# A transformer block with adaptive LayerNorm on one core: loads begun once per step, a fourth exp bank in some half-steps, and another order of the V tiles in the ramp

## The chip, the cores and the metric

The kernel runs on one core of one Trainium2 chip. The metric is the device time of one execution in microseconds (us); less is better. A core has five engines with instruction queues of their own: TensorE (PE in the profile, its weight loads PEld), VectorE (DVE), ScalarE (ACT), GpSimd (POOL) and SyncE (SP). SP only starts transfers here, one after the other, in the order of the program.

## What is computed

The input `x` has 2048 rows of 512 numbers, all in fp32. A vector `c` gives two shifts, two scales and two gates:

```python
mod = (_silu(c) @ w_mod).reshape(c.shape[0], 6, 1, -1)
sa, ca, ga, sb, cb, gb = (mod[:, i] for i in range(6))
h = _layernorm(x) * (1 + ca) + sa
x = x + ga * _A_ref(h, A_wqkv, A_wo)          # attention, 32 heads of 16 dims, no mask
h = _layernorm(x) * (1 + cb) + sb
x = x + gb * _B_ref(h, B_w1, B_b1, B_w2, B_b2)  # 512 -> 1792, gelu (tanh form), -> 512
```

Attention takes a softmax over all 2048 keys for each query, with the scale 1/4 on the scores.

## The kernel before

**Numbers.** Every fp32 operand of a large product is split into a high and a low part, and three products (high by high, low by high, high by low) are added in one PSUM bank. For the scores of a head of 16 dims the three are stacked along the contraction: 48 rows, and for the exp two more rows that carry minus the row maximum. So a score tile is one matmul, `mx` (line 393) with 48 rows and `e` (line 577) with 50.

**Units and half-steps.** Attention is cut into 32 units: 4 blocks of 512 queries by 8 groups of 4 heads. A unit has 16 steps of 128 keys. TensorE works on two halves of its rows, `a` = 0 and 1, with two heads of the unit in each. The loop runs over 512 pieces that the code calls half-steps (`half_step`, 16 to a unit); each is as long as a step, and from one to the next the row half in which a background product runs changes. A half-step has on TensorE:

- 4 matmuls `e`, whose exp ScalarE takes into tiles `p` (line 582). They go round the PSUM banks 0, 1 and 2.
- 4 matmuls `mx` for a later unit, whose maxima over 512 keys VectorE takes (line 398). They go round the banks 3, 4 and 5. When a unit's 64 reductions are done, `max_rows` turns them into rows and sends them over DRAM into the rows 48 and 49 of that unit's Q tile (`qst`, line 423).
- 4 matmuls `pv` (line 606): probabilities by V with a column of ones, into bank 6, one bank for the 16 half-steps of a unit. At a unit's end ScalarE copies it to `osb` (line 594), which goes to DRAM (`ou`).
- Where there is any, up to 6 matmuls of a background product into bank 7 (ring `bg`). In the first block of queries these are the Q and K projections of the later head groups (`block0`); then for each finished block the output projection, the second LayerNorm and the FFN (`ffn_block`).

A clock of the program, `clock["t"]`, counts exp tiles; `later(n, f)` writes the instructions of `f` down n ticks on. So the order on each engine is fixed when the program is built.

**Loads.** `step_start(s)` is called by `exp_mm` as a step begins. In step 1 of a unit it loads the first half of the keys of the unit after the next (`load_k`, line 364, 6 transfers into `kh`), in step 2 that unit's Q (`load_q`, line 379, 6 transfers into `qst`), in step 3 the next unit's V (`load_v`, line 529, one transfer into `vg`), in step 9 the second half of the keys. Every third step it also prepares a piece of the FFN's weights (`prep`), and it calls `try_prep`. The condition by which `exp_mm` calls it is

```python
if min(ec) == ec[a] and ec[a] % 2 == 0 and (a == 0 or ec[0] > ec[1]):
    step_start(s)
```

where `ec` counts the `e` of the two row halves; it is met a second time when the other half reaches the same step with the two counts level.

**The attention output.** `o_prep` (four times for a block) loads the row sums `dn` (line 636) and the outputs `ob` (line 639) back from DRAM. Ten ticks later VectorE takes the reciprocal of `dn` (line 646), which goes to DRAM and comes back spread over the rows as `rb`; GpSimd divides (line 658). The FFN's pools open (`open_ffn`) when the list of weights to prepare is empty, and `o_prep` begins after that.

**The ramp.** Ahead of the loop the four blocks of 512 rows go through: the first LayerNorm (`ln1`: statistics on VectorE, the factor by a power on GpSimd, line 232, scaling on ScalarE, line 249), its transposes (`ln1_t`: TensorE line 260, ScalarE line 266, high and low parts on GpSimd, lines 268 and 269, on VectorE too for the first block), the K projection (`proj_qk`, stored by line 308 and loaded back by `load_k`), and four V tiles (`proj_v`). From the second block on the V tiles are written as a `quad`: four groups in two banks' worth of row halves, with pairs of `mx` put between their matmuls, 2, 1, 1, 2, 1, 1, 2 and 1 pairs after every sixth index. The rows of block b lie in `xin[b % 2]`. After the last block a quad of K projections and the rest of 88 `mx` follow, and then the loop.

**The tail.** After half-step 511 the last block's output projection and FFN run by themselves.

Of the kernel before, what the change touches and what calls it, by code (L numbers as in the profile page):

```python
# [17 lines left out]
D = 512  # L18
# [4 lines left out]
KC = D // P  # L23
NB = 4
# [25 lines left out]
def block_kernel(ctx: ExitStack, tc: tile.TileContext, x, wqkv, wo, w1, b1, w2, b2, c, w_mod, out):  # L50
# [84 lines left out]
    def stage(name):  # L135
        return spool.tile([P, D], F32, tag="s2", name=name, bufs=4)
# [8 lines left out]
    def load_wm(i, slot):  # L145
        sy.dma_start(wslot[slot], wm_r[:, :, i * D : (i + 1) * D])

    def load_x(b):
        for t in range(4):
            r0 = b * TB + t * P  # L150
            sy.dma_start(xin[b % 2][:, t], x[r0 : r0 + P, :])
# [17 lines left out]
                ac.activation(t[:, 0, w], raw[:, w], AF.Copy)  # L169
                gp.tensor_tensor(t[:, 1, w], raw[:, w], t[:, 0, w].bitcast(F32), op=ALU.subtract)  # L170

    def load_split_v():
        for i in range(KC):
            r = stage("vraw")
            sy.dma_start(r, wq_r[:, i, 2 * D :])
            ac.activation(wv[:, 0, i], r, AF.Copy)
            eng = gp if i % 2 else ve
            eng.tensor_tensor(wv[:, 1, i], r, wv[:, 0, i].bitcast(F32), op=ALU.subtract)
# [3 lines left out]
    load_wm(1, 0)  # L182
    load_wm(0, 1)
    load_w(0)
    load_x(1)


    ac.activation(s_c, c_c, AF.Exp, scale=-1.0)
# [243 lines left out]
    def mx_pair():  # L432
        seen = [f() for f in [mx_mm(1), mx_mm(0)]][0]
        advance()
        return seen
# [4 lines left out]
    rows = ln1(0)  # L440
# [7 lines left out]
    mrow = mod_copy(psm)  # L448
    mod_cols(0, mrow)
    ev()  # L450
    load_split_v()
    sy.dma_start(one_d.rearrange("a (x y) -> a x y", y=128), ones[:, None, :].to_broadcast([2, HS // 128, 128]))
    def quad(groups, visits):

        at = [take(bk) for _, bk, _ in groups]
        seen, visits = {}, iter(visits)
        for phase in range(2):
            for two in ((0, 1), (2, 3)):
                for m in range(12):
                    for i in two:  # L460
                        h = phase ^ (i % 2)
                        terms = groups[i][0]
                        ins = mm(at[i], terms[m], 12 * phase + m, 24, slice(h * 64, h * 64 + 64)).ins
                        if phase and not m:
                            tc.add_manual_dep(ins, seen[two].name, AFTER, reason="both halves of the rows add to one bank")
                        if phase and m == 11:
                            groups[i][2](at[i])
                    if m % 6 == 5:
                        for n in range(next(visits)):
                            ins = mx_pair()  # L470
                            if not n and m == 11:
                                seen[two] = ins.ins

    for b in range(NB):
        if b + 1 < NB:
            rows = ln1(b + 1)
        run(proj_qk("pr", 1, 0, b, fast=True))
        if b == 0:
            run(proj_qk("pr", 0, 0, 0, fast=True))
        for u in range(2):  # L480
            if u == 0 or b < 2:
                load_k(u, b // 2, (b % 2) * TB, (b % 2 + 1) * TB)
            if b == 0:
                load_q(u)
        if b + 2 < NB:
            load_x(b + 2)
        if b == 0:
            load_w(1)
            load_wm(4, 0)
            load_wm(3, 1)  # L490
        if b + 1 < NB:
            ln1_t(b + 1, rows)()
        if b == 1:
            split_w(1)
            psm = take("pr")
            mod_part(psm, 0)
            mod_part(psm, 1)
            mrow = mod_copy(psm)
            mod_cols(1, mrow)
            load_wm(2, 0)  # L500
            load_wm(5, 1)
        if b == 3:
            psm = take("pr")
            mod_part(psm, 0)
            mod_part(psm, 1)
            mrow = mod_copy(psm)
            mod_bcast((ga_b, gb_b), mrow)
        tiles = [proj_v("pr", b, t) for t in range(4)]
        if b:
            quad(tiles, (2, 1, 1, 2, 1, 1, 2, 1))  # L510
        else:
            for t in tiles:
                run(t)
        if b + 1 == NB:
            sy.dma_start(b2_b, bass.AP(tensor=b2.tensor, offset=b2.offset, ap=[[0, P], [1, D]]))
            sy.dma_start(b1_h, b1.rearrange("(f p) -> p f", p=P))
# [12 lines left out]
        sy.dma_start(vg[u], v_d[u % NG])  # L529

    load_v(0)
    quad([proj_qk("pr", 1, 1, b) for b in range(NB)], (2, 1, 1, 2, 1, 1, 2, 1))
    run(proj_qk("pr", 0, 1, 0))
    ac.activation(b1_h, b1_h, AF.Copy, scale=0.5)
    gp.tensor_tensor(b2_b, b2_b, gb_b, op=ALU.mult)
# [25 lines left out]
    ring("mx", (3, 4, 5))  # L561
    ring("pv", (6,))
    ring("bg", (7,))
    ec = [0, 0]
    cur = {"pv": 0}

    def exp_mm(a):

        s, p = divmod(ec[a], 2)
        if min(ec) == ec[a] and ec[a] % 2 == 0 and (a == 0 or ec[0] > ec[1]):  # L570
            step_start(s)
        ec[a] += 1
        u, kc = divmod(s, NKC)
        assert u in mrows, (u, ec, xc, red, clock["t"])
        r0 = a * 64
        ps = take("e")
        te.matmul(ps, kh(u, kc // 8)[r0 : r0 + KX, p, (kc % 8) * P : (kc % 8 + 1) * P], qst[u][r0 : r0 + KX, p],  # L577
                  start=True, stop=True)

        def act():  # L580
            t = ppool.tile([P, TB], F32, tag="p", name="p")
            saw(ac.activation(t, ps, AF.Exp, scale=SCALE))  # L582
            pt[4 * s + p * 2 + a] = t
            advance()

        return act
# [302 lines left out]
    def half_step(hs):  # L889
        h = hs % 2  # L890
        if h:
            wload()
        if act["g"] is None:
            j = next(jobs, None)
            if callable(j):
                j()
            elif j is not None:
                act["g"] = {"group": j, "at": [0, 0], "n": 0, "seen": None}
        nx = min(64 * NU, LEAD + 4 * (hs + 1))
        ne = 4 * (hs + 1)  # L900

        def x_ok(a):
            return sum(xc) < nx and xc[a] < 32 * NU

        def e_ok(a):
            return sum(ec) < ne and ec[a] < 2 * NU * NKC

        more = act["g"] is not None
        k = 0
        while more and k < RUN:  # L910
            a = 1 - h
            more = bg_mm(h)
            if e_ok(a) and sum(ec) < ne - 1 and (k % 2 == 1 or not x_ok(a)):
                exp_mm(a)()
            elif x_ok(a):
                mx_mm(a)()
            k += 1
        while sum(ec) < ne or sum(xc) < nx:
            a = 0 if ec[0] <= ec[1] else 1
            fs = []  # L920
            if sum(ec) < ne:
                fs.append(exp_mm(a))
                if x_ok(1 - a):
                    fs.append(mx_mm(1 - a))
                elif e_ok(1 - a):
                    fs.append(exp_mm(1 - a))
            else:
                fs += [mx_mm(i) for i in range(2) if x_ok(i)]
            for f in fs:
                f()  # L930
        if hs:
            assert min(ec) >= 2 * cur["pv"] + 2
            pv_step()
# [86 lines left out]
```

## Time and profile before

| | |
|---|---|
| three runs | 1872.36, 1882.72, 1886.42 us |
| median | 1882.72 us |
| profiled execution | 1873.15 us, of which the span of the trace is 1871.3 |
| mean granted TensorE clock | 0.966 of full |
| busy: PE, DVE, ACT, POOL | 1757.6, 1404.0, 1212.9, 601.3 us |
| as shares of the span | 94%, 75%, 65%, 32% |
| transfers | 279.09 MB, 149 GB/s on the mean |

The costliest groups of instructions, with the idle time ahead of them and what ended most of it:

```profile
L398 DVE TENSOR_REDUCE mxp<-mx 128x1 f32<-128x512 f32 x2048 | 1273.6, 681 | 222.9 <-PE mx L393 192.1
L582 ACT ACTIVATE p<-e 128x512 f32<-128x512 f32 x2048 | 1070.3, 603 | 397.8 <-PE e L577 334.3
L393 PE MATMUL mx<-kh,qst 48*128 48x512 f32 x2048 | 877.2, 446 | 37.3 <-DVE mxp L398 36.4
L577 PE MATMUL e<-qst,kh 50*128 50x512 f32 x2048 | 761.9, 425 | 25.2 <-ACT p L582 17.3
L606 PE MATMUL pv<-p,vg 128*32 128x512 f32 x4096 | 557.6, 617 | 0.0
```

How to read such rows. A group's row has its line, engine, operation, the tile written and the tiles read with partitions and elements, the count, then busy microseconds, mean nanoseconds of one, and the idle time of the engine just before. Busy times of TensorE add up instructions that overlap in its pipeline, so its share says little by itself. A row of one instruction begins with its start and its duration in microseconds; in brackets stand the engine's idle time just before it and what ended that. The row of a stretch (`440.00:462.00`) has its length, then for PE, PEld, DVE, ACT and POOL the busy time and in brackets the number of instructions, then the granted TensorE clock, the busy share of the transfer engines and the GB/s. The chain (the row of `PE 76%`) follows the last instruction back, at each step to what released it. DMA rows with SPq have the start and the time on SP's queue.

### The profile page before, as it was taken

The page shows a single profiled execution, that of the slowest core. Times are in us where ns is not written, and L with a number is a line of the kernel's source. Part 1 is how long each engine was busy: PE and PEld are TensorE (multiplying, and loading weights), DVE is VectorE, ACT ScalarE, POOL GpSimd, SP SyncE. Part 2 cuts the span into 40 slices and gives each one's busy share as a digit, 9 for nine tenths or more (in the row PEclk, how much of TensorE's full clock was granted, in tenths as well). Part 3 has the DMA queues.
Part 4 walks back from the last instruction along what each step waited for, and adds up shares of the span by engine and source line. Part 5 has one row for each costly group of instructions (what it writes and reads, how often), then busy time and mean ns, then how long its engine had stood idle before and what let it go on. Part 6 is the DMA issues. An engine that isn't in the chain of part 4 may idle for free.

```text
span 1871.3 us, 32540 instructions
## 1 busy us (share of the span) xinstructions
PE 1757.6 (94%) x12032; PEld 905.2 (48%) x12032; DVE 1404.0 (75%) x2347; ACT 1212.9 (65%) x2303; POOL 601.3 (32%) x640
## 2 busy tenths in 40 slices
PE   7698999998888899999999989999999999999899
PEld 5465444443333444444444444444444444444677
DVE  4466888887787978888888988888889878860232
ACT  3223777777565678778766668777776668777031
POOL 3213545442100146405510046504510046504520
PEclk8898999999899999999999999999999999999899
DMA  5828778777775467767767754435547457612544
GB/s 168 245 84 203 200 195 215 198 205 158 187 152 111 109 131 158 146 113 181 177 138 175 197 115 109 98 87 142 115 91 194 75 135 159 146 61 91 186 158 157
DMA packets 135292, 279.09 MB, mean 149 GB/s; under 512 B 34598, under 2 KB 54070, under 8 KB 135134
## 3 DMA queue, kind: packets, MB, share of 16 engines
q1 hardware_dynamic: 135134, 277.02, 61.4%
q8 instruction: 95, 1.56, 0.4%
q14 instruction: 63, 0.52, 0.1%
HBM read 224.04 MB, written 52.90 MB: 148 GB/s over the span
## 4 chain that ended last, share of the span: by engine, by line
PE 76%; DMA 8%; DVE 8%; ACT 3%; issue 2%; SPq 2%; POOL 1%; DVEq 0%; ACTq 0%; POOLq 0%
PE bg L287 34%; PE pv L606 23%; PE e L577 11%; DVE mxp L398 5%; PE mx L393 4%; PE pr L287 3%; DMA kh<-qk 2%; DMA dn<-ou 2%; ACT p L582 1%; DVE bst L227 1%; DVE x L818 1%; DMA vg<-v 1%; SPq L364 1%; DMA wraw<-in_A_wqkv_dram 1%; DMA rden<-dn 0%
## 5 line engine op out<-in xcount | busy, mean ns | idle before, releaser
L398 DVE TENSOR_REDUCE mxp<-mx 128x1 f32<-128x512 f32 x2048 | 1273.6, 681 | 222.9 <-PE mx L393 192.1
L582 ACT ACTIVATE p<-e 128x512 f32<-128x512 f32 x2048 | 1070.3, 603 | 397.8 <-PE e L577 334.3
L393 PE MATMUL mx<-kh,qst 48*128 48x512 f32 x2048 | 877.2, 446 | 37.3 <-DVE mxp L398 36.4
L577 PE MATMUL e<-qst,kh 50*128 50x512 f32 x2048 | 761.9, 425 | 25.2 <-ACT p L582 17.3
L606 PE MATMUL pv<-p,vg 128*32 128x512 f32 x4096 | 557.6, 617 | 0.0
L577 PEld LDWEIGHTS e<-qst,kh 50*128 50x128 f32 x2048 | 377.5, 189 | 228.8 <-ACT p L582 194.4
L393 PEld LDWEIGHTS mx<-kh,qst 48*128 48x128 f32 x2048 | 378.9, 189 | 64.0 <-DVE mxp L398 57.2
L287 PE MATMUL bg<-w,g 64*128 64x512 f32 (+1 forms) x1020 | 276.5, 408 | 3.4 <-DVE x L818 1.0
L287 PE MATMUL bg<-pc,w 64*128 64x512 f32 (+1 forms) x984 | 270.6, 408 | 1.4 <-DVE x L818 0.7
L287 PEld LDWEIGHTS bg<-w,g 64*128 64x128 f32 (+1 forms) x1020 | 179.8, 187 | 146.7 <-ACT p L582 82.7
L287 PEld LDWEIGHTS bg<-pc,w 64*128 64x128 f32 (+1 forms) x984 | 169.5, 184 | 159.9 <-ACT p L582 98.8
L606 PEld LDWEIGHTS pv<-p,vg 128*32 128x32 f32 x4096 | 81.2, 108 | 130.4 <-issue 123.6
L412 POOL CAST m<-mt 128x32 fp32r<-128x32 f32 x32 | 6.7, 210 | 323.8 <-DVE mt L410 323.8
L287 PE MATMUL bg<-hThi,wqk 64*128 64x512 f32 x352 | 107.2, 424 | 0.3 <-ACT p L582 0.3
L792 POOL TENSOR_SCALAR s<-s 128x512 f32<-128x512 f32 x42 | 63.0, 1499 | 132.1 <-ACT s L790 124.2
L287 PEld LDWEIGHTS bg<-hThi,wqk 64*128 64x128 f32 x352 | 59.5, 188 | 80.2 <-ACT p L582 71.5
L287 PE MATMUL bg<-wo,pc 64*128 64x512 f32 x288 | 82.8, 414 | 3.7 <-DMA wo<-wos 1.6
L658 POOL TENSOR_TENSOR ob<-ob,rb 128x512 f32<-128x512 f32 x12 | 15.4, 1284 | 219.0 <-DMA rb<-rden 146.7
L785 POOL TENSOR_TENSOR s<-h 128x512 f32<-128x512 f32 x42 | 43.7, 1039 | 120.7 <-ACT h L784 120.5
L287 PEld LDWEIGHTS bg<-wo,pc 64*128 64x128 f32 x288 | 50.1, 187 | 52.0 <-ACT p L582 28.5
L322 POOL CAST parts<-pf 128x512 fp32r<-128x512 f32 x27 | 16.5, 610 | 153.1 <-ACT pf L321 149.7
L646 DVE RECIPROCAL dn<-dn 128x32 f32<-128x32 f32 x16 | 5.6, 347 | 71.1 <-DMA dn<-ou 69.7
(125 smaller groups left out, 1212.2 us busy)
## 6 DMA issues: line engine op xcount, KB each, us to landing
kh<-qk SPq DMA_DIRECT2D x546, 128.0 KB
vg<-v SPq DMA_DIRECT2D x48, 664.0 KB
w<-w1s SPq DMA_DIRECT2D x56, 512.0 KB
w<-w2s SPq DMA_DIRECT2D x51, 512.0 KB
qk<-parts SPq DMA_DIRECT2D x32, 512.0 KB
qst<-qk SPq DMA_DIRECT2D x222, 64.0 KB
ou<-osb SPq DMA_DIRECT2D x32, 256.0 KB
wo<-wos SPq DMA_DIRECT2D x15, 512.0 KB
```

Of the source, the lines that this page charges most:

```text
L227: ve.bn_stats(st, rows)
L287: return te.matmul(ps, term[0][r], term[1][r], start=i == 0, stop=i == n - 1)
L322: gp.tensor_copy(parts[:, 0], r)
L364: sy.dma_start(kh(u, h)[r0 : r0 + DH, :, t0:t1].bitcast(F32), heads(1, u % NG, part, a, h * HS + t0, h * HS + t1))
L393: te.matmul(ps, qst[u][r0 : r0 + KR, p, qc * P : (qc + 1) * P], kh(u, kr // 2)[r0 : r0 + KR, p, (kr % 2) * TB : (kr % 2 + 1) * TB], start= ...
L398: ins = ve.tensor_reduce(mxp[u][:, hc, kr : kr + 1], ps, axis=AX.X, op=ALU.max, negate=True)
L577: te.matmul(ps, kh(u, kc // 8)[r0 : r0 + KX, p, (kc % 8) * P : (kc % 8 + 1) * P], qst[u][r0 : r0 + KX, p], start=True, stop=True)
L582: saw(ac.activation(t, ps, AF.Exp, scale=SCALE))
L606: te.matmul(cur["ps"][32 * j : 32 * (j + 1)], vg[u][:, kc, j * VW : j * VW + 32], pt.pop(4 * s + j), start=kc == 0, stop=kc == NKC - 1)
L785: gp.tensor_tensor(s, h, h, op=ALU.mult)
L792: gp.tensor_scalar(s, s, 1.0, None, op0=ALU.add)
L818: ve.tensor_tensor(x2[t], ps, x2[t], op=ALU.add)
```

## The change

It has three parts.

**1. Each step's loads are begun once.** A counter `begun` says how many steps have been started; `exp_mm` calls `step_start` once for each. The line numbers of the main part move by 11 or 12.

**2. A fourth exp bank.** In a half-step that begins without a background product the last of its four `e` is taken from the ring `bg`, which is bank 7. In the other half-steps nothing changes.

**3. The ramp.** V's weights are loaded into `xin[1]` early, where the second block's rows were loaded, and are split from there. The second block's rows are loaded after the first 24 transfers of K and Q. The V tiles of the first block come ahead of the second block's LayerNorm. The statistics of block b + 2 move from the start of the next round into the quad of block b, behind its fifth pair of `mx` (for block 0 behind its tiles). The quads take one pair of `mx` after every fourth index, eleven times, instead of eleven pairs in eight places.

```diff
-    def load_split_v():
+    def split_v():
         for i in range(KC):
-            r = stage("vraw")
-            sy.dma_start(r, wq_r[:, i, 2 * D :])
+            r = xin[1][:, i]
             ac.activation(wv[:, 0, i], r, AF.Copy)
...
     load_w(0)
-    load_x(1)
+    for i in range(KC):
+        sy.dma_start(xin[1][:, i], wq_r[:, i, 2 * D :])
...
-    load_split_v()
+    split_v()
...
-                    if m % 6 == 5:
-                        for n in range(next(visits)):
-                            ins = mx_pair()
-                            if not n and m == 11:
-                                seen[two] = ins.ins
+                    if m % 4 == 3:
+                        f = next(visits)
+                        if f:
+                            ins = f()
+                        if m == 11:
+                            seen[two] = ins.ins
 
     for b in range(NB):
-        if b + 1 < NB:
-            rows = ln1(b + 1)
         run(proj_qk("pr", 1, 0, b, fast=True))
...
             if b == 0:
                 load_q(u)
+        if b == 0:
+            load_x(1)
         if b + 2 < NB:
             load_x(b + 2)
...
+        tiles = [proj_v("pr", b, t) for t in range(4)]
+        if b == 0:
+            for t in tiles:
+                run(t)
+            rows = ln1(1)
         if b + 1 < NB:
             ln1_t(b + 1, rows)()
...
-        tiles = [proj_v("pr", b, t) for t in range(4)]
         if b:
-            quad(tiles, (2, 1, 1, 2, 1, 1, 2, 1))
+            def both():
+                nonlocal rows
+                seen = mx_pair()
+                if b + 2 < NB:
+                    rows = ln1(b + 2)
+                return seen
+
+            quad(tiles, [mx_pair] * 4 + [both] + [mx_pair] * 6 + [None])
         else:
-            for t in tiles:
-                run(t)
+            rows = ln1(2)
...
-    quad([proj_qk("pr", 1, 1, b) for b in range(NB)], (2, 1, 1, 2, 1, 1, 2, 1))
+    quad([proj_qk("pr", 1, 1, b) for b in range(NB)], [mx_pair] * 11 + [None])
...
-    ec = [0, 0]
+    ec, begun = [0, 0], [0]
...
-    def exp_mm(a):
+    def exp_mm(a, bk="e"):
 
         s, p = divmod(ec[a], 2)
-        if min(ec) == ec[a] and ec[a] % 2 == 0 and (a == 0 or ec[0] > ec[1]):
-            step_start(s)
+        while begun[0] < min(ec) // 2 + 1:
+            begun[0] += 1
+            step_start(begun[0] - 1)
         ec[a] += 1
...
-        ps = take("e")
+        ps = take(bk)
...
         more = act["g"] is not None
+        free = not more
...
-                fs.append(exp_mm(a))
+                fs.append(exp_mm(a, "bg" if free and sum(ec) == ne - 1 else "e"))
```

What this does to the order on the engines shows at three places. A row has the line, the operation, the tile written and the tiles read (a number tells copies of a tile apart), the shape and how often it stands in a row.

SP in the ramp, from the early loads on. Before:

```order
L151 DMA xin_210<-in_A_x_dram 128x512 x4
L175 DMA vraw<-in_A_wqkv_dram 128x512 x4
L452 DMA one<-ones 16x1x128
L308 DMA qk_87<-parts 128x2x512
L308 DMA qk_83<-parts 128x2x512
L364 DMA kh_190<-qk_87 16x2x512 x6
L379 DMA qst<-qk_83 16x2x512 x6
L364 DMA kh_192<-qk_87 16x2x512 x6
L379 DMA qst<-qk_83 16x2x512 x6
L151 DMA xin_209<-in_A_x_dram 128x512 x4
```

And of the change:

```order
L185 DMA xin_210<-in_A_wqkv_dram 128x512 x4
L452 DMA one<-ones 16x1x128
L308 DMA qk_87<-parts 128x2x512
L308 DMA qk_83<-parts 128x2x512
L364 DMA kh_190<-qk_87 16x2x512 x6
L379 DMA qst<-qk_83 16x2x512 x6
L364 DMA kh_192<-qk_87 16x2x512 x6
L379 DMA qst<-qk_83 16x2x512 x6
L151 DMA xin_210<-in_A_x_dram 128x512 x4
L151 DMA xin_209<-in_A_x_dram 128x512 x4
```

The second block's rows (`xin_210`, four transfers) moved from ahead of the K and Q round trip to behind it; V's weights took their place.

VectorE around the quad of the second block (from the first reductions of `mx` to the second group of them). Before:

```order
L398 TENSOR_REDUCE mxp<-mx 128x1 x22
L227 BN_STATS bst<-xin_210 128x6
L228 BN_AGGR mv<-bst 128x2
...
L231 TENSOR_SCALAR rs<-mv 128x4
L246 TENSOR_TENSOR nb<-mv,rs 128x4
L247 TENSOR_SCALAR nb<-nb 128x4
L318 TENSOR_TENSOR parts<-pr,parts 128x512
```

And of the change:

```order
L398 TENSOR_REDUCE mxp<-mx 128x1 x10
L227 BN_STATS bst<-xin_210 128x6
L228 BN_AGGR mv<-bst 128x2
...
L231 TENSOR_SCALAR rs<-mv 128x4
L246 TENSOR_TENSOR nb<-mv,rs 128x4
L247 TENSOR_SCALAR nb<-nb 128x4
L398 TENSOR_REDUCE mxp<-mx 128x1 x12
L318 TENSOR_TENSOR parts<-pr,parts 128x512
```

The statistics of the fourth block's rows stood behind all 22 reductions of the quad; now they stand behind 10 of them, and 12 wait behind them.

SP where the FFN opens and the first `o_prep` begins. Before:

```order
L364 DMA kh_191<-qk_87 16x2x1024 x12
L595 DMA ou_124<-osb 128x512
L379 DMA qst<-qk_83 16x2x512 x12
L731 DMA x_5906<-in_A_x_dram 128x512
...
L731 DMA x_5909<-in_A_x_dram 128x512
L529 DMA vg<-v 128x1328
L636 DMA dn<-ou_124 128x1x32
L639 DMA ob<-ou_124 64x1x512 x2
L529 DMA vg<-v 128x1328
```

And of the change:

```order
L364 DMA kh_191<-qk_87 16x2x1024 x6
L607 DMA ou_124<-osb 128x512
L379 DMA qst<-qk_83 16x2x512 x6
L540 DMA vg<-v 128x1328
L561 DMA w2s_164<-wsp 128x1024
L743 DMA x_5923<-in_A_x_dram 128x512
...
L743 DMA x_5926<-in_A_x_dram 128x512
L648 DMA dn<-ou_124 128x1x32
L651 DMA ob<-ou_124 64x1x512 x2
```

The 12 transfers of K and the 12 of Q became 6 and 6, the second load of `vg` is gone, and the store of the last prepared weight (`w2s_164`) now stands behind the load of V.

## Prediction

> **What bounds the kernel now.** I read the page's chain first, then the transfers' list, then the time at which each unit of attention ends, then the idle times of VectorE (DVE) and TensorE (PE).
>
> ```profile
> PE 76%; DMA 8%; DVE 8%; ACT 3%; issue 2%; SPq 2%; POOL 1%; DVEq 0%; ACTq 0%; POOLq 0%
> ...
> kh<-qk SPq DMA_DIRECT2D x546, 128.0 KB
> vg<-v SPq DMA_DIRECT2D x48, 664.0 KB
> ```
>
> TensorE carries three quarters of the chain, but 8% of 1871.3 us is transfers, some 150 us in a kernel whose loads are meant to be far ahead. The counts say why: 32 units need 32 loads of `vg`, not 48, and 61 half loads of K with 6 transfers each, 366, not 546. The rest are loads begun twice.
>
> A row per unit (16 half-steps) comes from the copy of its result by ScalarE (ACT):
>
> ```profile
> 448.84 0.60 ACT L594 ACTIVATE osb<-pv 128x512 f32<-128x512 f32 x1 [0.28 <-PE pv L606]
> ...
> 612.63 0.60 ACT L594 ACTIVATE osb<-pv 128x512 f32<-128x512 f32 x1
> ...
> 902.66 0.62 ACT L594 ACTIVATE osb<-pv 128x512 f32<-128x512 f32 x1
> ...
> 1055.77 0.60 ACT L594 ACTIVATE osb<-pv 128x512 f32<-128x512 f32 x1
> ...
> 1297.96 0.60 ACT L594 ACTIVATE osb<-pv 128x512 f32<-128x512 f32 x1
> ...
> 1439.29 0.60 ACT L594 ACTIVATE osb<-pv 128x512 f32<-128x512 f32 x1
> ```
>
> Each pair is 48 half-steps apart: 163.79, 153.11 and 141.33 us. All three hold the preparation of one block's attention output (`o_prep`, four times). In the first two loads are begun twice, in the third none is (no load is doubled between steps 298 and 432). The third is my control: 2.94 us a half-step, mostly with background products.
>
> **Part 1: loads begun once.** Before the change `step_start` runs again when the second half of the rows reaches a step whose first half is only one ahead. In the program 30 half loads of K, 5 of Q and 16 of V are doubled: 180 + 30 + 16 = 226 transfers go. What they cost stands where the first `o_prep` runs:
>
> ```profile
> 444.21 8.66 SPq L364 DMA_DIRECT2D kh<-qk  x12
> ...
> 453.40 10.64 SPq L379 DMA_DIRECT2D qst<-qk  x12
> 464.08 1.85 SPq L731 DMA_DIRECT2D x<-in_A_x_dram  x4
> ...
> 466.44 0.65 SPq L636 DMA_DIRECT2D dn<-ou  x1
> ```
> ```profile
> 472.17 0.35 DVE L646 RECIPROCAL dn<-dn 128x32 f32<-128x32 f32 x1 [11.25 <-DMA dn<-ou]
> ...
> 577.42 0.35 DVE L646 RECIPROCAL dn<-dn 128x32 f32<-128x32 f32 x1 [5.67 <-DMA dn<-ou]
> ```
> ```profile
> 440.00:462.00 22.00, 20.24 (x136) 7.71 (x128) 18.86 (x31) 17.09 (x34) 1.65 (x2) 1.00 0.76 137
> 462.00:474.00 12.00, 1.77 (x12) 0.97 (x5) 1.83 (x4) 0.86 (x2) 0.00 (x0) 0.61 0.68 212
> ```
>
> The small load `dn` waits on SP's queue behind 12 transfers of K, 12 of Q and 4 of x. It lands 5.7 us after its issue. The reciprocal stands in VectorE's order between the reductions of `mx`, so 11.25 us of its waiting stop the reductions, then the `mx` banks, then TensorE, whose clock (the column after the counts) falls to 0.61 of full and is slow for some us after.
>
> With single loads SP takes 2.7 us for six of K and 2.8 for six of Q (the ramp's rows below give 2.66 for the first six and 11.1 for 24), 1.85 for x, and 1 to 2 for what lies between. `dn` is then issued about 453 and lands near 459. The reciprocal is reached at 460.93 (472.17 less 11.25), and since the preparation opens one half-step later (step 100, not 99), at 463.7. So the wait goes, with some 4 us of margin. Likewise at 577.42: in the program's order the same 12 and 12 stand ahead of `dn`, and half of them, as at 444.21 and 453.40, is 8.66 + 10.64 - 5.4 = 13.9 us of SP against a wait of 5.67. What is late next is the row sums' next consumer, `ob`, on GpSimd, which nothing in that stretch waits for.
>
> First stretch: 41 of its 48 half-steps have no background product and take 2.74 us (rows of part 3), 7 take 2.94: 132.9 us. Measured 163.79, so 30.9 too long; by an estimate 1.4 of it is VectorE's adds of the output projection in the last ones, which stay. I take -29.5. Second stretch against the control: 153.11 - 141.33 = 11.8, of which I leave 1.3 to the same adds: -10.5. Cover gone: if the loads are late for another reason, both come back. The last block's doubles (steps 433 to 511) stop nothing that I can find: 0.
>
> **Part 2: the ramp.** V's weights take the early place of x(1), and x(1) goes behind the first 24 loads of K and Q.
>
> ```profile
> 35.72 0.97 SPq L308 DMA_DIRECT2D qk<-parts  x2
> 38.61 2.66 SPq L364 DMA_DIRECT2D kh<-qk  x6
> ...
> 49.70 1.84 SPq L151 DMA_DIRECT2D xin<-in_A_x_dram  x4
> ```
> ```profile
> 24.59 1.07 PE L287 MATMUL pr<-hTlo,wqk 128*128 128x512 f32 x4
> ...
> 59.09 0.47 PE L260 MATMUL pr<-ident,xin 128*128 128x128 f32 x1 [7.29 <-ACT xin L249]
> ...
> 71.13 0.50 PE L393 MATMUL mx<-kh,qst 48*128 48x512 f32 x1 [0.56 <-DVE mxp L398]
> ...
> 92.13 0.33 PE L260 MATMUL pr<-ident,xin 128*128 128x128 f32 x1 [4.03 <-ACT xin L249]
> ...
> 153.30 0.49 PE L393 MATMUL mx<-kh,qst 48*128 48x512 f32 x1 [0.57 <-DVE mxp L398]
> 164.39 0.76 PE L577 MATMUL e<-qst,kh 50*128 50x512 f32 x1 [5.37 <-issue]
> ```
> ```profile
> 56.73 1.01 POOL L232 TENSOR_TENSOR rs<-rs,mhalf 128x4 f32<-128x4 f32 x1 [12.81 <-DVE rs L231]
> ...
> 62.56 0.61 POOL L268 CAST hThi<-h 128x512 fp32r<-128x512 f32 x1 [4.82 <-ACT h L266]
> ...
> 68.96 1.29 POOL L269 TENSOR_TENSOR hTlo<-h,hThi 128x512 fp32r<-128x512 f32 x1
> ```
> ```profile
> 86.20 0.68 DVE L227 BATCH_NORM_STATS2 bst<-xin 128x6 f32<-128x512 f32 x1
> ...
> 91.00 0.17 DVE L247 TENSOR_SCALAR nb<-nb 128x4 f32<-128x4 f32 x1
> ```
> ```profile
> 85.10:97.20 12.10, 7.24 (x29) 5.30 (x28) 5.44 (x14) 6.38 (x10) 2.53 (x3) 0.81 0.79 212
> ```
>
> The second product ends at 25.66. Its parts and the first's no longer queue on ScalarE behind x(1), so the stores leave by about 24 and 27 instead of 35.72; a store takes 2.9 to land (38.61 - 35.72), and the 24 loads run from about 27 to 38 (11.1 us, as from 38.61 to 49.70). TensorE does the V tiles meanwhile. x(1) is issued near 38.3. From issue to transposes took 59.09 - 49.70 = 9.4, so these start near 47.7, late. Hi and lo of the block begin 3.5 after (62.56 - 59.09), at 51.2, and take GpSimd 7.7 (62.56 to 70.25). In the new order the factor of the next LayerNorm comes behind that on GpSimd, at 58.9, and its transposes 2.4 later (59.09 - 56.73), at 61.3 instead of 59.09: +2.2.
>
> From there the change earns it back. The third LayerNorm's 5.0 us on VectorE (86.20 to 91.17) moves inside the tiles of the second block, where by an estimate the `mx` banks run dry for 2.8 of them: +2.8. The wait before the transposes of x(3) goes: -4.0. The clock of 0.81 around it rises, 7.24 busy us times 0.19: -1.4. And 12 waits for VectorE of 0.52 to 0.57, where two pairs of `mx` stood together (first and last shown), go when single pairs are spread out: -6.5. Sum -6.9. The first `e` at 164.39 waits for the row maxima, whose way over SP begins with the end of the V tiles and moves with it. I take -7, between -12 (the early lateness is hidden) and +7 (x(3) too lands late, and the banks stay dry for its landing).
>
> **Part 3: a fourth exp bank.** A half-step without background product:
>
> ```profile
> 530.27 0.50 PE L577 MATMUL e<-qst,kh 50*128 50x512 f32 x1
> ...
> 530.80 2.06 ACT L582 ACTIVATE p<-e 128x512 f32<-128x512 f32 x4 [0.68 <-PE mx L393]
> 530.84 2.48 DVE L398 TENSOR_REDUCE mxp<-mx 128x1 f32<-128x512 f32 x4 [0.25 <-PE mx L393]
> ...
> 531.45 0.50 PE L577 MATMUL e<-qst,kh 50*128 50x512 f32 x1 [0.21 <-ACT p L582]
> ...
> 531.58 0.50 PE L393 MATMUL mx<-kh,qst 48*128 48x512 f32 x1
> ...
> 532.01 1.07 PE L606 MATMUL pv<-p,vg 128*32 128x512 f32 x8
> ...
> 533.00 0.18 PEld L577 LDWEIGHTS e<-qst,kh 50*128 50x128 f32 x1 [0.84 <-ACT p L582]
> ```
>
> The period is 533.01 - 530.27 = 2.74. The fourth `e` at 531.45 waits for the first exp's bank, and this wait goes. But the fourth `mx` behind it has three banks too, and needs the first reduction, which ends near 531.53. It starts 0.05 later, and `pv` 0.43 after that. This loop closes by itself: 0.43 + 0.99 (`pv`) + 0.57 (to the reduction) + 0.69 + 0.05 = 2.73. So 0 of 2.74. Of 512 half-steps 81 have no background product, 69 of them plain and 12 with transposes for the second LayerNorm, by the program's order. Bounds: below, the 0.13 between the two starts in 69, -9, if nothing but the `e` held the loop; above, +2, for the 12, where transposes share bank 7 with the exp of the half-step before, and with them the `e` and `mx` queued behind them on TensorE wait, an estimated 0.1 to 0.2 each.
>
> **Sum.** 1873.15 (the profiled execution: 1871.3 and 1.85 around it) - 29.5 - 10.5 - 7 + 0 = 1826. That execution lies 9.6 under the median 1882.72; two of three runs were near 1882 to 1886, and what makes them longer may partly stay, so I say **1829**.
>
> **Rivals.** (a) *The wait moves.* `dn` is early, but the preparation's other loads (weights of 512 KB, `m` rows) still hold SP; half of part 1 stays: 1829 + 20 = 1849. For: the opening is a half-step later, with the last prepared weight's store just ahead of x on SP. Against: the control's four preparations stop nothing. (b) *The bank pays.* If ScalarE's loop alone set 2.74, it would end at VectorE's 2.48 for four reductions: 69 x 0.26 = 18 less, 1811. Against: the 0.05 above. (c) *The doubles were hidden*, and 472.17 waited for bandwidth: only the ramp, 1873 - 7 = 1866. Against: 11.25 us with TensorE idle. (d) *Slower: the clock.* One row stands against the change:
>
> ```profile
> 1488.70:1499.00 10.30, 10.30 (x42) 3.72 (x38) 7.89 (x14) 5.28 (x11) 2.72 (x3) 0.50 1.04 148
> ```
>
> Here TensorE shows no idle time, in half-steps without background, and yet runs at half clock, and x42 matmuls in 10.30 us against x136 in 22.00 make a half-step 1.52 times as long, 4.15 us. With the fourth `e` early, TensorE's wait before the fourth `mx` becomes one piece of about 0.5 us instead of 0.21 and less. If that halves the clock through the 46 half-steps 92 to 137, it costs 46 x 1.41 = 65: 1894. It decides from (1882.7 - 1829) / 1.41 = 38 such half-steps on. Against: 440 to 462 holds the same loop at clock 1.00.
>
> The Trainium skill, "TensorE: Matmul & The Clock Gate", section "A second HAM failure mode: psum-queue depth-cycling", describes such a case: short idles between groups that cycle through PSUM banks make the clock swing. By that rule (d) would be likelier; the trace shows it in one stretch and not in the other. Its section "HAM oscillation — how this bites in real kernels" allows idle gaps up to about 3.4 us, and by that one (d) would not happen; the fall at 462 behind a longer gap agrees with it.
>
> **How the numbers follow.** Forecast 0.67, (a) 0.15, (b) 0.06, (c) 0.07, (d) 0.05. The range 1812 to 1852 holds the bounds of the ramp, (b)'s edge and (a). A measurement here tells apart about 1%, 18.8 us. Faster than 1863.9 are the forecast, (a) and (b), with a little of (c): 0.89; same 0.07; slower 0.04.
>
> **What would show it.** Right: 366 transfers of `kh` and 32 of `vg`; no reciprocal of `dn` in the main part waiting over 2 us; the first stretch's 48 half-steps in about 134 us, the second's in 143; plain half-steps still 2.74; first `e` near 157. Wrong: 2.74 turned to 2.5 (b), clock at 0.5 between 440 and 570 (d), or reciprocals that still wait (a).

## The result and the profile after

The changed kernel takes 1829.83 us in the median of 4 runs (1825.15 to 1833.69), against 1881.88 in the median of 4 runs of the kernel before. The ratio is 0.9729, with an interval of 0.9683 to 0.9774. Its profiled execution took 1831.95 us, 41.2 less than the one of before.

The loads are begun once. The list of transfers of the changed kernel:

```profile
kh<-qk SPq DMA_DIRECT2D x366, 128.0 KB
...
vg<-v SPq DMA_DIRECT2D x32, 664.0 KB
```

The copies of the units' results, as in the prediction, for the first and the second stretch of 48 half-steps:

```profile
439.95 0.60 ACT L606 ACTIVATE osb<-pv 128x512 f32<-128x512 f32 x1 [0.28 <-PE pv L618]
...
579.12 0.60 ACT L606 ACTIVATE osb<-pv 128x512 f32<-128x512 f32 x1
...
871.26 0.62 ACT L606 ACTIVATE osb<-pv 128x512 f32<-128x512 f32 x1
...
1013.31 0.60 ACT L606 ACTIVATE osb<-pv 128x512 f32<-128x512 f32 x1
```

The first stretch fell from 163.79 to 139.17 us (-24.6), the second from 153.11 to 142.05 (-11.1), as good as the control's 141.33. What is left over in the first stands at its first reciprocal. SP, VectorE and a stretch of the changed kernel:

```profile
444.28 0.38 SPq L561 DMA_DIRECT2D w2s<-wsp  x1
451.14 1.76 SPq L743 DMA_DIRECT2D x<-in_A_x_dram  x4
452.94 0.65 SPq L648 DMA_DIRECT2D dn<-ou  x1
```
```profile
456.82 0.35 DVE L658 RECIPROCAL dn<-dn 128x32 f32<-128x32 f32 x1 [2.05 <-DMA dn<-ou]
```
```profile
457.00:466.00 9.00, 8.22 (x31) 3.62 (x31) 6.79 (x12) 4.23 (x8) 0.00 (x0) 0.54 0.68 198
```

SP has nothing to do from 444.66 to 451.14: the loads of `x` wait there, behind the store of the last prepared weight, and `dn` stands behind them. The reciprocal still waits 2.05 us, and TensorE runs at 0.54 of its clock for the next 9 us.

The ramp on TensorE, at the places that the prediction named:

```profile
48.79 0.47 PE L260 MATMUL pr<-ident,xin 128*128 128x128 f32 x1 [11.39 <-ACT xin L249]
...
62.25 0.33 PE L260 MATMUL pr<-ident,xin 128*128 128x128 f32 x1 [0.69 <-ACT xin L249]
...
84.36 0.79 PE L393 MATMUL mx<-kh,qst 48*128 48x512 f32 x1 [4.64 <-DVE mxp L398]
...
156.37 0.76 PE L589 MATMUL e<-qst,kh 50*128 50x512 f32 x1 [4.80 <-issue]
```

The second block is late (TensorE waits 11.39 us for it), the statistics inside the quad cost 4.64, and yet the first `e` comes 8.0 us earlier, at 156.37. The twelve waits of 0.52 to 0.57 and the 4.03 us before the transposes of x(3) are gone, but they alone do not make up for both; the whole account stands further down.

A half-step without background product, TensorE:

```profile
510.67 0.50 PE L589 MATMUL e<-qst,kh 50*128 50x512 f32 x1
...
511.48 0.39 PE L589 MATMUL bg<-qst,kh 50*128 50x512 f32 x1
511.99 0.50 PE L393 MATMUL mx<-kh,qst 48*128 48x512 f32 x1
...
513.41 0.50 PE L589 MATMUL e<-qst,kh 50*128 50x512 f32 x1
```

The fourth `e` (into bank 7) starts 0.81 us behind the first instead of 1.18. The fourth `mx` starts 1.32 behind it, as before (1.31), and the half-step still takes 2.74.

### The profile page after: what moved, and what is told of

Its sections match the earlier page's. It is cut to its first block, busy times and chain, and to the rows that moved or that the text cites. A ratio compares the mean times of both kernels' runs of the same rounds, so it can differ in the third digit from the quotient of the medians.

```text
span 1829.8 us, 32358 instructions
## 1 busy us (share of the span) xinstructions
PE 1752.0 (96%) x12032; PEld 905.0 (49%) x12032; DVE 1403.7 (77%) x2347; ACT 1210.8 (66%) x2303; POOL 602.5 (33%) x640
## 5 line engine op out<-in xcount | busy, mean ns | idle before, releaser
L594 ACT ACTIVATE p<-e 128x512 f32<-128x512 f32 x1967 | 1029.4, 603 | 358.8 <-PE e L589 305.4
L589 PE MATMUL e<-qst,kh 50*128 50x512 f32 x1967 | 716.9, 419 | 5.1 <-issue 4.8
L589 PEld LDWEIGHTS e<-qst,kh 50*128 50x128 f32 x1967 | 359.7, 188 | 173.3 <-ACT p L594 150.8
L287 PE MATMUL bg<-hThi,wqk 64*128 64x512 f32 x352 | 107.2, 424 | 0.3 <-ACT p L594 0.3
L773 ACT ACTIVATE h<-bg,modc 128x512 f32<-128x512 f32 x16 | 12.1, 778 | 67.5 <-PE bg L771 41.7
L807 POOL TENSOR_TENSOR g<-h,g 128x512 fp32r<-128x512 f32 x42 | 53.9, 1284 | 3.4
```

The costliest lines, as they stand in the source:

```text
L287: return te.matmul(ps, term[0][r], term[1][r], start=i == 0, stop=i == n - 1)
L773: ac.activation(h, ps, AF.Identity, scale=modc[:, 1, fc, 0:1], bias=modc[:, 1, fc, 1:2])
L807: gp.tensor_tensor(g[:, 1], h, g[:, 0].bitcast(F32), op=ALU.subtract)
```

## The experiments

**The parts one by one.** Part 1 alone in the kernel before:

```diff
-    ec = [0, 0]
+    ec, begun = [0, 0], [0]
...
-        if min(ec) == ec[a] and ec[a] % 2 == 0 and (a == 0 or ec[0] > ec[1]):
-            step_start(s)
+        while begun[0] < min(ec) // 2 + 1:
+            begun[0] += 1
+            step_start(begun[0] - 1)
```

> The kernel before with part 1 of the change alone. My theory: the doubled transfers cost time only by holding up the small load of the row sums on SP, so VectorE's reciprocals stop the reductions. It expects some 36 us less than before (about 25 in half-steps 92 to 137, 11 in the second block's four preparations), near 1846, with the first e still near 165. Rival, the gain comes from the fourth bank or from the ramp: no more than 10 us less, and half-steps 92 to 137 as long as before (155.6 us).

It took 1836.63 us (before in the same session 1876.99), a ratio of 0.9788 (0.9769 to 0.9806): 40 us less. The first stretch took 138.95 us and the second 142.31, as in the whole change. The gain of the main part is part 1's.

Part 3 alone, the ramp as in the diff of the change:

> The kernel before with part 3 alone (V's weights early, the other order of the first two blocks, single pairs of mx). My theory: the first e 8 us earlier (near 157), everything behind it as before, so 8 to 9 us less than before. Rival, the earlier start is eaten by a later wait in the first block of queries: the first e earlier, the time within 3 us of before.

The first `e` came at 158.66 us. The time was 1871.99, a ratio of 0.9981 (0.9958 to 1.0004), 3.6 us less, with an interval from 8 less to 1 more. Behind the ramp its first stretch took 168.87 us instead of 163.79 (a reciprocal that waited 2.60 us where it had waited 1.95, another 1.52 where it had not waited), so much of the gain was given back. Over all kernels run, the first `e` comes at 164.4 to 166.5 us with the old ramp (4 executions, mean 165.4) and at 155.6 to 163.1 with the new one (10, mean 158.0): the ramp's own gain is 7.3 us, and one execution alone says it to some 4.

The change without part 2:

```diff
-                fs.append(exp_mm(a, "bg" if free and sum(ec) == ne - 1 else "e"))
+                fs.append(exp_mm(a))
```

> The changed kernel without part 2: the fourth exp of a half-step without background product stays in the ring of three banks. My theory: plain half-steps take 2.74 us with and without it, because the mx banks close the loop; the time stays within 4 us of the changed kernel, 1830. Rival, the bank pays: plain half-steps longer by about 0.13 to 0.26, and 9 to 18 us more, 1839 to 1848. Second rival, the bank costs in the half-steps with transposes: 2 to 4 us less.

It took 1835.43 us, ratio to before 0.9777 (0.9755 to 0.9799), which does not differ clearly from the change's 0.9729. TensorE in it:

```profile
525.88 0.50 PE L589 MATMUL e<-qst,kh 50*128 50x512 f32 x1
...
527.06 0.50 PE L589 MATMUL e<-qst,kh 50*128 50x512 f32 x1 [0.21 <-ACT p L594]
528.62 0.50 PE L589 MATMUL e<-qst,kh 50*128 50x512 f32 x1
```

Plain half-steps take 2.74 us without the bank too (528.62 - 525.88). Of the 5.0 us between the two profiled executions 5.1 stand before the first `e` (161.45 against 156.37), where their programs are the same. The bank is worth nothing that shows.

**Was it the place of `dn` on SP's queue?** In the kernel before, `dn` was given to GpSimd's queue; the doubled loads stay:

```diff
-        sy.dma_start(dn, base[2 * k : 2 * k + 2]...)
+        gp.dma_start(dn, base[2 * k : 2 * k + 2]...)
```

> The kernel before, with one edit: the load of the row sums (dn) is issued by GpSimd's queue instead of SP's. All 226 doubled transfers stay. My theory, the queue: the first reciprocal waits under 3 us instead of 11, half-steps 92 to 137 fall from 155.6 us to 126 to 135, the second block's preparations by about 10, the whole by 25 to 36. Rival, bandwidth: the doubled transfers slow the small load wherever it is issued, the reciprocals still wait over 5 us, and the time stays within 8 us of before.

The time did not fall: 1881.84, ratio 1.0036 (1.0011 to 1.0060). VectorE and GpSimd in it:

```profile
462.65 0.34 DVE L646 RECIPROCAL dn<-dn 128x32 f32<-128x32 f32 x1
497.71 0.35 DVE L646 RECIPROCAL dn<-dn 128x32 f32<-128x32 f32 x1 [18.34 <-DMA dn<-ou]
```
```profile
484.44 1.26 POOL L658 TENSOR_TENSOR ob<-ob,rb 128x512 f32<-128x512 f32 x1 [40.09 <-DMA rb<-rden]
...
487.65 0.63 POOL L636 DMA_DIRECT2D dn<-ou  x1
```

The first reciprocal no longer waits, as expected. But the second `dn` stands on GpSimd behind the first division, and that waits for `rb`, which SP brings late behind the doubled loads. I had not followed the second `dn` past GpSimd's own queue. So `dn` went to ScalarE's queue (the same edit with `ac`), where only exps are ahead of it:

> The kernel before with the load of the row sums (dn) issued by ScalarE's queue, where only exps stand ahead of it; all 226 doubled transfers stay on SP. It mends the last try, where the second and third dn stood behind a division on GpSimd's queue. My theory, the place on the queue is what costs: no reciprocal of the main part waits over 1 us, half-steps 92 to 137 take 126 to 132 us instead of 155.6, the whole is 25 to 38 us less than before. Rival, the doubled transfers as such (bandwidth, or the stores and loads of rb and ob behind them on SP): reciprocals go through, but another wait of over 5 us takes their place and the time stays within 12 us of before.

Now no reciprocal waits, and the kernel is slower than before: 1899.39, ratio 1.0105 (1.0072 to 1.0139). TensorE, SP and GpSimd in it:

```profile
520.49 0.76 PE L577 MATMUL e<-qst,kh 50*128 50x512 f32 x1 [20.19 <-DMA qst<-m]
```
```profile
504.19 2.64 SPq L364 DMA_DIRECT2D kh<-qk  x6
...
513.55 1.19 SPq L417 DMA_DIRECT2D m<-m  x2
...
518.81 0.57 SPq L423 DMA_DIRECT2D qst<-m  x2
```
```profile
501.81 0.25 POOL L413 TENSOR_TENSOR m<-mt,m 128x32 fp32r<-128x32 f32 x1
```

The `e` of a new unit waits 20.19 us for its row maxima. VectorE had them at 475.78. GpSimd's work on them ended only at 502.06, since it stands there behind the first division, which began at 498.29: the `rb` that it divides by had left SP at 493.75. Then their store left SP at 513.55, behind six transfers of K (504.19), and their load at 518.81. So two queues held them up, GpSimd's and SP's, and SP was late in both cases. My theory in its narrow form fell here: `dn` was the first to suffer from a full queue, and not the only one. With `dn` out of the way the maxima were next. One thing stays open. The twelve transfers of K and of Q ahead of this took SP 13.32 and 20.33 us, more than the 8.66 and 10.64 before; why is not shown.

**Place, or bytes?** The change with the 226 transfers back, as copies into DRAM that nothing reads, at the places of the doubled loads, once on SP and once on GpSimd:

```diff
+    def copy(src, shape):
+        extra_n[0] += 1
+        sy.dma_start(dram.tile(shape, F32, name=f"again{extra_n[0]}"), src)
...
+        if min(ec) == ec[a] and ec[a] % 2 == 0 and (a == 0 or ec[0] > ec[1]):
+            if s in met:
+                again(s)
+            met.add(s)
```

> The changed kernel with the 226 transfers back as copies of the same sources into DRAM nobody reads, issued on SP at the places of the doubled loads. They wait for nothing but their place. Theory A, the length of SP's queue: most of the 36 us comes back (20 to 40 more than the changed kernel, 1850 to 1870), with waits of VectorE for dn or of SP's own stores and loads of the maxima. Theory B, what cost was that a doubled load waits on SP until the first copy has landed: these copies wait for nothing, so under 12 us more. Theory C, the transfer engines' time: as A, and the next run too.

> The same 226 copies, issued on GpSimd's queue instead of SP's. Theory A (SP's queue): under 10 us more than the changed kernel, unless GpSimd's own work (maxima, divisions) is held up, which its waits would show. Theory B: under 10 more too. Theory C (the transfer engines are what is short): within 8 us of the run with the copies on SP, 20 to 40 more than the changed kernel.

On SP: 1847.42 us, ratio to before 0.9828 (0.9797 to 0.9860). On GpSimd: 1832.51, ratio 0.9763 (0.9718 to 0.9807). Against the change's 0.9729 that is 18.6 us more on SP and 6.4 on GpSimd, where the interval takes in zero. The first reciprocal of each (first SP, then GpSimd), and SP in the first:

```profile
463.20 0.35 DVE L682 RECIPROCAL dn<-dn 128x32 f32<-128x32 f32 x1 [9.08 <-DMA dn<-ou]
```
```profile
461.37 0.35 DVE L682 RECIPROCAL dn<-dn 128x32 f32<-128x32 f32 x1 [6.62 <-DMA dn<-ou]
```
```profile
434.69 2.66 SPq L364 DMA_DIRECT2D kh<-qk  x6
437.40 3.97 SPq L580 DMA_DIRECT2D again<-qk  x6
```

The same bytes cost about half of the 36 us that the two stretches had lost when they stand on SP's queue, and little beside it. The first stretch takes 13.9 us more than in the change with the copies on SP, 3.1 with the copies on GpSimd, where what shows of them is one wait of 6.62 us: traffic alone can make `dn` late once. These copies work by another way than the doubled loads did. On SP they put the last weight's store off from 444.28 to 451.04, and the loads of `x`, with `dn` behind them, wait for it.

The other half has a likely cause in the waits of SP in the kernel before (in all, how often, the longest):

```profile
SPq L364 <- DMA kh<-qk: 97.9, 124, 6.2
...
SPq L529 <- DMA vg<-v: 56.4, 15, 5.0
```

A load of K waits for a load of K to land, a load of V for a load of V. With 13.6 us of the same for Q this is 168 us of SP's time, and in the change and in both kernels with copies no such wait shows. So a doubled load waits on SP until the first has landed, and what stands behind it waits too. Twelve transfers of K took SP 8.66 us before; six and six copies take 6.63 here. That these waits are the other half is not shown: no kernel tried them alone. Part 1 also lets the FFN open a half-step later, which no run separates from the loads.

**What sets 2.74?** The eight `pv` matmuls ahead of the fourth pair of a half-step without background product:

```diff
+        early = False
         while sum(ec) < ne or sum(xc) < nx:
+            if free and hs and not early and sum(ec) == ne - 1:
...
+                pv_step()
+                early = True
...
-        if hs:
+        if hs and not early:
```

> The changed kernel, but in half-steps without background product the eight pv matmuls stand ahead of the fourth e and mx instead of behind them. My theory of the 2.74 us is that the loop over three mx banks closes it (the fourth mx waits for the first reduction, pv for that mx); with pv put into that wait, VectorE's four reductions are the next bound, 2.48 us: 0.26 less in about 69 half-steps, 10 to 18 us less than the changed kernel. Rival, ScalarE's or VectorE's own rate sets 2.74: no difference. Second rival, the clock falls as TensorE's waits come in one piece: slower.

1829.77 us, ratio 0.9741 (0.9709 to 0.9773): no difference. TensorE:

```profile
517.54 0.50 PE L393 MATMUL mx<-kh,qst 48*128 48x512 f32 x1
...
520.28 0.50 PE L393 MATMUL mx<-kh,qst 48*128 48x512 f32 x1
```

The period is 520.28 - 517.54 = 2.74 again. Here I had drawn the wrong conclusion from my own loop: wherever `pv` stands, four `mx` on three banks lie between one `pv` and the next, and the last of them starts 1.3 us behind the first. So the fourth bank was given to `mx`:

```diff
-    def mx_mm(a):
+    def mx_mm(a, bk="mx"):
...
-        ps = take("mx")
+        ps = take(bk)
...
-                fs.append(exp_mm(a, "bg" if free and sum(ec) == ne - 1 else "e"))
+                fs.append(exp_mm(a))
                 if x_ok(1 - a):
-                    fs.append(mx_mm(1 - a))
+                    fs.append(mx_mm(1 - a, "bg" if free and sum(ec) == ne else "mx"))
```

> The changed kernel, with bank 7 given to the fourth mx of a half-step without background product instead of the fourth e. Both tries on the 2.74 us so far (a fourth exp bank; pv ahead of the fourth pair) left it. My theory: between one pv and the next stand four mx on three banks, in any order, and the fourth waits for the first one's reduction (1.31 us behind the first start); with a fourth bank the e loop is next, whose fourth starts 1.18 behind the first: 2.61 us, 0.13 less in about 69 half-steps, 5 to 9 us less. Rival, an engine's own pace sets 2.74: no change of the plain half-steps.

TensorE:

```profile
508.99 0.49 PE L589 MATMUL e<-qst,kh 50*128 50x512 f32 x1
...
510.17 0.50 PE L589 MATMUL e<-qst,kh 50*128 50x512 f32 x1 [0.21 <-ACT p L594]
...
511.60 0.50 PE L589 MATMUL e<-qst,kh 50*128 50x512 f32 x1
```

The period is 2.61, as the loop says, with the fourth `e` 1.18 behind the first and now the one that waits. No engine's own pace sets it. The whole kernel took 1829.08, ratio 0.9729 (0.9708 to 0.9750): the gain of some 6 us in 46 half-steps does not stand out of the spread.

**Towards a faster one.** The FFN's loads of `x` behind the first division:

```diff
+        if not tail:
+            yield from until(lambda: done[b] >= 0)
         for t in range(4):
             r0 = b * TB + t * P
             sy.dma_start(x2[t], x[r0 : r0 + P, :])
```

> The changed kernel, with the four loads of x for the FFN behind the first division instead of ahead of the first dn. My theory: these loads wait on SP for the store of the last prepared weight (their tiles lie where its source lay), and dn behind them; without them ahead the first reciprocal's wait of 2.05 us goes, and with it the half clock of half-steps 103 to 105 (4.71, 4.23 and 4.20 us instead of 2.74): 5 to 8 us less than the changed kernel, 1822 to 1825. Rival, dn is late for its own way through DRAM: the wait stays, no difference.

1834.19 us, ratio 0.9771 (0.9732 to 0.9810): nothing gained. The first reciprocal does not wait. SP has the reason:

```profile
470.01 4.44 SPq L745 DMA_DIRECT2D x<-in_A_x_dram  x4
474.94 0.60 SPq L648 DMA_DIRECT2D dn<-ou  x1
```

The loads now stand ahead of the second `dn`, whose reciprocal waits 3.58 us. The wait had moved by one, and the first stretch takes 139.37 us, as in the change (139.17).

The scaling of the second LayerNorm on GpSimd:

```diff
-        yield from wait(7)
+        if tail:
+            yield from wait(7)
...
-            ve.tensor_scalar(xn[t], x2[t], mv[:, t, 0:1], rs[:, t : t + 1], op0=ALU.subtract, op1=ALU.mult)
-            gp.tensor_tensor(x2[t], x2[t], b2_b, op=ALU.add)
-        yield from wait(4)
+            (ve if tail else gp).tensor_scalar(xn[t], x2[t], mv[:, t, 0:1], rs[:, t : t + 1], op0=ALU.subtract, op1=ALU.mult)
+            if tail:
+                gp.tensor_tensor(x2[t], x2[t], b2_b, op=ALU.add)
+        yield from wait(4 if tail else 11)
...
+            for t in range(4):
+                gp.tensor_tensor(x2[t], x2[t], b2_b, op=ALU.add)
```

The wait of 7 ticks that stood ahead of the scaling now stands behind it, and the adds of `b2` come behind the transposes.

> The changed kernel, with the scaling of the second LayerNorm (four operations for each of three blocks) on GpSimd instead of VectorE, and the adds of b2 behind the transposes. My theory: in the changed kernel these four operations hold VectorE for 3.7 us, the mx banks run dry, TensorE idles 3.5 us and then runs at half clock for some 10 us; nine half-steps take 35 to 37 us instead of 25. Without them on VectorE each of the three places falls by 8 to 12 us: 24 to 36 us less, 1794 to 1806. Rival, the transposes wait for GpSimd instead: under 10 us less. Second rival, the half clock comes by itself there, whatever VectorE does: the stall of 3.5 us goes three times, 10 us less, but the clock of 0.5 stays.

1815.66 us, ratio 0.9662 (0.9626 to 0.9697): 14 us less than the change. In the change, VectorE, TensorE and a stretch:

```profile
617.97 3.80 DVE L764 TENSOR_SCALAR xn<-x,mv,rs 128x512 f32<-128x512 f32 x4
```
```profile
622.42 0.79 PE L393 MATMUL mx<-kh,qst 48*128 48x512 f32 x1 [3.48 <-DVE mxp L398]
```
```profile
622.00:635.00 13.00, 12.50 (x55) 5.33 (x57) 7.13 (x12) 5.54 (x10) 5.89 (x6) 0.62 0.13 25
```

The same stretch with the scaling on GpSimd:

```profile
622.00:635.00 13.00, 12.59 (x76) 5.59 (x72) 8.88 (x15) 10.17 (x19) 6.83 (x8) 1.00 0.49 81
```

The clock is back at 1.00. The nine half-steps around each of the three places fell by 6.6, 5.3 and 5.4 us, fewer than I expected, because the half-steps with transposes take 3.5 us in any case. Part of this may be chance: the three places together take 107.2 us in the change, the most of all kernels with this scaling on VectorE (97.7 to 107.2), and 89.9 here.

All three together, with the loads of `x` behind the last division:

> The changed kernel with the three edits that the runs point to: bank 7 for the fourth mx instead of the fourth e, the second LayerNorm's scaling on GpSimd, and the FFN's loads of x behind the last division of a block instead of ahead of the first dn. By the runs so far: plain half-steps 2.61 us; 5 to 6 us less at each of the three second LayerNorms; no reciprocal of the main part waiting over 0.5 us and no half clock behind it, 5 to 8 less in half-steps 102 to 137. Sum 25 to 32 us less than the changed kernel: 1798 to 1805. Rival, the loads of x now come late for the output projection, or the waits move to the next load: 1810 or more.

1817.16 us, ratio 0.9672 (0.9642 to 0.9701): the same as the scaling alone. The first stretch is nearly as hoped, 2.61 a half-step and no half clock; one reciprocal still waits, 1.15 us. GpSimd, TensorE and a stretch at the second LayerNorm:

```profile
604.40 8.26 POOL L767 TENSOR_SCALAR xn<-x,mv,rs 128x512 f32<-128x512 f32 x4
```
```profile
612.72 0.33 PE L775 MATMUL bg<-ident,xn 128*128 128x128 f32 x1 [1.68 <-POOL xn L767]
```
```profile
612.00:628.00 16.00, 14.51 (x67) 5.94 (x67) 7.98 (x13) 9.80 (x18) 6.41 (x8) 0.68 0.34 56
```

With shorter half-steps the same wait of 11 ticks is shorter than GpSimd's 8.26 us. The transposes begin 6.12 us behind the scaling's start (610.52 against 604.40), where they had 7.78 in the run before (622.12 against 614.34); they come too early, and the clock falls again. A longer wait was not tried.

## Why the prediction was right, and where it was not

- **Part 1, first stretch, -29.5: measured -24.6.** The step that failed is the margin of "some 4 us" for `dn`. I had it issued some 4 us behind the copy of the unit's result (453 against 448.84) and the reciprocal 14.9 behind (463.7). The reciprocal was reached 14.8 behind (454.77 against 439.95), as said; but `dn` was issued 13.0 behind (452.94), since SP stood for 6.5 us on the last weight's store. The wait of 2.05 us, and half clock behind it, are the 4.9 us missing (half-steps 103 to 105 take 4.71, 4.23 and 4.20 us instead of 2.74). Two of my own signs were missed by this: no reciprocal over 2 us, and about 134 us for the stretch, which took 139.17. Rival (a) had named this cause and priced it at 20.
- **Second stretch, -10.5: measured -11.1.** The control served well.
- **The ramp, -7: measured -8.0**, 7.3 over all executions. Its terms were off and made up for each other. The second block's lateness brings the third block's transposes at 62.25 instead of 59.09, +3.2 for +2.2. The quad with the statistics takes 4.6 more (21.25 us from 71.28 on, 16.63 from 68.45 on before) although its three waits of 0.5 are gone, so the statistics cost some 6 for the 2.8 that I had estimated. Against that, 4.2 go ahead of the fourth block's transposes (those of x(3); I took 4.0), and these take 1.84 instead of 5.07, 3.2 less for 1.4. The stretches of the later quads take 3.3 and 4.2 less, more than their nine waits.
- **The bank, 0: measured 0**, for the reason given. Rival (b) falls: an `mx` bank brings 2.61, an `e` bank nothing. In the twelve half-steps with transposes the `e` bank costs 0.04 each (3.53 against 3.49), less than the 0.1 to 0.2 that I had allowed, and the half-step behind them is 0.16 shorter (2.46 against 2.62).
- **Rival (c)**, that the doubled loads were hidden: wrong, by part 1 alone.
- **Rival (d)**, the clock: no fall through the stretch from 440 to 570 apart from the 9 us behind the reciprocal. The row at 1488.70 that spoke for it I had cut too short: TensorE waits 0.75 us ahead of the `mx` at 1487.01, just before it. The second rule of the Trainium skill, "TensorE: Matmul & The Clock Gate", section "HAM oscillation — how this bites in real kernels", was the better guide to that, though not in its figure (below).
- **The mechanism** was right in the large: the doubled loads' place on SP's queue. As I told it, with `dn` as the thing that is late, it was too narrow; the runs put the row maxima and `rb` beside it. And about half of the cost is not the place of so many transfers but, I think, the wait of each doubled load for the first, which SP's waits show and no run priced.
- **The number.** The sum said 1826.15 for an execution like the one profiled, which took 1831.95; 4.9 of these 5.8 us are the first stretch; the second stretch and the ramp gave 1.6 more than forecast, and changes elsewhere took 2.5 (the three second LayerNorms alone 2.8: 107.2 us for 104.4). The 3 us that I added for the median, and the other three executions (1825.15 to 1833.69), bring 1829 so near to 1829.83. That is closer than the working deserves.

## What to carry to other kernels

Count the transfers against what the algorithm needs before looking at any wait: 48 loads of V for 32 units told most of this case. When one queue is too full, the operation seen waiting on it is only the first; here moving that one to another queue uncovered the next, and only taking work off the queue helped. When a loop has the same period after two different edits, write down everything between two turns of the same bank before trying a third.

## What the runs showed of the hardware that I had not expected

TensorE's clock falls after idle times far below a loop's length, and not by their size alone. TensorE in the kernel with part 1 alone, and in the one with the scaling on GpSimd, each with the stretch behind it:

```profile
469.22 0.50 PE L393 MATMUL mx<-kh,qst 48*128 48x512 f32 x1 [0.69 <-DVE mxp L398]
```
```profile
469.00:481.00 12.00, 11.78 (x47) 4.11 (x47) 9.14 (x17) 6.10 (x12) 3.20 (x4) 0.63 0.77 181
```
```profile
478.95 0.49 PE L393 MATMUL mx<-kh,qst 48*128 48x512 f32 x1 [0.76 <-DVE mxp L398]
```
```profile
478.90:490.00 11.10, 10.73 (x63) 4.34 (x63) 10.34 (x17) 7.75 (x15) 0.00 (x0) 1.00 0.48 142
```

After 0.69 us of idle time the clock is 0.63 over 12 us, after 0.76 it stays at 1.00; and in the change without the fourth bank 0.34 us of idle time (ahead of 464.17) were followed by a clock of 0.63 over 14 us. What decides is not shown. In the first of these kernels the wait was 1.72 us on VectorE, and half-steps 103 to 106 take 3.89, 3.92, 4.19 and 4.18 us instead of 2.74: 5.2 us in all, most of it half clock. The section of the Trainium skill named above speaks of idle gaps over about 3.4 us; here falls came behind far shorter ones.

VectorE's scaling slows down beside GpSimd: the first two of the four `xn` operations take 0.54 us each, the other two 1.49 and 1.48, while GpSimd adds (1.50 and 1.44 each). The Trainium skill, "SBUF — State Buffer", section "Terms", has the two engines share a port pair that one of them holds for a whole instruction; the trace agrees. The third operation starts at 618.87 and ends at 620.36, just behind GpSimd's first add (618.58 to 620.08).
